# Attention with a gated MLP on one core: seventeen of 31 normalising products move from VectorE to GpSimd, and the planner's numbers are set anew

## The chip, the cores and the metric

The kernel runs on one core of one Trainium2 chip. The metric is device time in microseconds (us) of one execution, and lower is better. Several engines of the core work side by side, each through its own list of instructions in order: TensorE (PE) for matrix products, ScalarE (ACT) for activation functions, VectorE (DVE) and GpSimd (POOL) for elementwise work, SyncE (SP) for issuing DMAs. They meet only at semaphores.

## The reference

Attention with 32 heads of 20 columns over 2048 tokens, an MLP with the mish activation, and a gate per token that mixes the two:

```python
def _A_ref(x, wqkv, wo):
    B, S, D = x.shape                      # 1, 2048, 640
    H = 32; Dh = D // H
    qkv = ((x @ wqkv).reshape(B, S, 3, H, Dh)).transpose(2, 0, 3, 1, 4)
    q, k, v = qkv[0], qkv[1], qkv[2]
    p = softmax(einsum("bhqd,bhkd->bhqk", q, k) * Dh ** -0.5)
    o = einsum("bhqk,bhkd->bhqd", p, v)
    return o.transpose(0, 2, 1, 3).reshape(B, S, D) @ wo

def _B_ref(x, w1, b1, w2):                 # 640 -> 1536 -> 640
    h = x @ w1 + b1
    return (h * tanh(softplus(h))) @ w2

g = sigmoid((x * gate_w).sum(-1, keepdims=True))
out = g * _A_ref(x, wqkv, wo) + (1 - g) * _B_ref(x, w1, b1, w2)
```

All inputs are bf16.

## The kernel before

**Tiling.** The queries are cut into four blocks of 512 (`c`), the heads into eight groups of four (`g`), the keys into 16 tiles of 128. One unit is one head's score block: 128 keys by 512 queries, one matmul (L1204). There are 2048 units, and they go in slots of three, 683 slots in all. PE writes the three score blocks of a slot into one of two halves of six PSUM banks. ACT takes the exponential of all three in one instruction, 128 × 1536 (L1226), into one of six buffers `ETS`, and PE multiplies them by the values and sums them in the accumulator bank (L1463). The scores of slot s+2 need the half that slot s has left.

**Off-loaded units.** In about three slots of five, DVE takes the third unit: ACT's exp is then short, 128 × 1024, and DVE *evicts* the third block out of PSUM (`emit_x`, helper `dve_by`, L1271) as int16 numbers whose bits approximate an exponential. Up to four such units make a batch, and a batch needs three further DVE steps in SBUF (`close`): a bit operation on 2048 columns (`fraction`, L1335), a product (`times_y`, L1339, in one piece of 2048 or two of 1024) and a second bit operation (`power`, L1343). So each off-loaded unit shortens ACT's work and lengthens DVE's. Which slots have one is decided by `choose`, which weighs what DVE still owes (`late`, `urgent`, `other`) against limits such as `BEHIND` and `IDLE`, with a correction per eight slots from the table `NUDGE`.

**Normalising.** After the last key tile of a group (c, g), `group_done` (L1500) copies the accumulator to `OUNG` (L1552), which also holds the softmax sums. A DMA collects the sums in `RR`, DVE inverts them (`invert`, L1574), a DMA writes them to DRAM, and four DMAs spread them over the partitions in `BCT` (`spread`, L1581). Then one product, `OUNG` by `BCT`, 128 × 512 in fp32 to bf16, gives the normalised output in `OTN` or, for the later half of the queries, in `QT` (`times`, L1513). There are 31 of these products; the last two half groups take another way. The next group's copy to `OUNG` must wait for the product. The output projection (L1048) reads the products of all eight groups.

**The MLP.** Its tanh runs on ACT (L983, 24 pieces of 128 × 1024), the polynomial behind it on DVE in eight pieces (`mish`, L1005 and L1008).

**What sets the order.** A planner in Python writes all five instruction lists. It keeps a planned clock for each engine (`pl.now`), gives every instruction a planned cost (`WIDE` 0.60, `QUICK` 0.335, `EXP` 1.335, ...) and adds waits from the dependencies. Work of PE beside the scores (projections, MLP) stands in `tasks` with due slots; some are forced. DVE's work falls into two sorts: evictions out of PSUM, placed at once, and pieces in SBUF, kept in queues (`norm` for normalising, `soon` for batches, `blend` for the MLP, `bg`) from which `work` takes the next whenever the planned clock leaves room before the next eviction. GpSimd has only set-up work at the start and one addition at the end.

A second list of instructions for inputs that the approximation doesn't cover stands behind a flag and isn't run here.

## Time and profile before

| | us |
|---|---|
| median of three runs | 789.43 (788.85 to 789.61) |
| the profiled execution | 789.46 |
| its span, first to last instruction | 787.6 |
| mean granted TensorE clock | 0.998 of full speed |

The span is what the views below cut up; 1.9 us of the profiled execution lie outside of it. A view by groups gives for each group of instructions its line, engine, operation, tiles written and read with shapes, count, then busy time and the mean of one in ns, then the engine's idle time before them and who ended it. A timeline row is start, duration, engine, line, operation, tiles, count. L-numbers are lines of the kernel before. Consecutive instructions of ACT and of DVE overlap a little in the records, since each is recorded until its last result has been written.

DVE's 31 normalising products, and the POOL work that there is:

```profile
L1513 DVE TENSOR_TENSOR QT<-OUNG,BCT 128x512 bf16<-128x512 f32 x15 | 10.2, 681 | 0.0
L591 POOL MEMSET QT<- 128x2048 bf16 x7 | 12.3, 1808 | 0.0
L554 POOL MEMSET V_all<- 128x512 bf16 x1 | 2.4, 2361 | 0.0
BCT<-SUMS SPq DMA_DIRECT2D x124, 64.0 KB, 2.1
```

The last row is the spreading of the reciprocals: 124 DMAs, each landing 2.1 us after its issue in the median.

### The profile page before, as it was taken

What the parts mean: (1) busy time and instruction counts of PE and PEld (TensorE: products, weight loads), DVE (VectorE), ACT (ScalarE), POOL (GpSimd) and SP (SyncE); (2) the same over time, 40 slices, a digit from 0 to 9 for tenths busy, and PEclk for the clock granted to TensorE, in tenths of its full rate; (3) what the DMA queues carried; (4) which work ended last, traced back from release to release, by engine and by line L of the source; (5) the groups of instructions that cost most, each with busy time, mean ns of one, the idle gap of its engine ahead of it and who ended that gap; (6) DMA issues with size and microseconds to landing.
All of it is one profiled execution on the core that took longest, in us unless ns stands there. A gap on an engine that the chain in (4) does not pass through costs nothing.

```text
span 787.6 us, 16572 instructions
## 1 busy us (share of the span) xinstructions
PE 721.0 (92%) x6711; PEld 264.4 (34%) x6711; DVE 754.4 (96%) x1358; ACT 771.0 (98%) x715; POOL 20.3 (3%) x21
## 2 busy tenths in 40 slices
PE   8999999989899988999999999899989999989996
PEld 4333333233223333233333333333333333333332
DVE  4899999999999999999999999999999999999996
ACT  6999999999999999999999999999999999999995
POOL 8100000000000000000000000000000000000000
PEclk9999999999999999999999999999999999999999
DMA  8221310311233212402131201301121212101101
GB/s 188 75 60 53 100 54 15 94 59 53 66 104 84 65 51 73 129 15 52 52 80 51 69 22 51 85 16 45 47 85 50 82 44 56 32 23 28 25 20 39
DMA packets 77800, 47.13 MB, mean 60 GB/s; under 512 B 23916, under 2 KB 73700, under 8 KB 77668
## 3 DMA queue, kind: packets, MB, share of 16 engines
q1 hardware_dynamic: 77316, 45.80, 21.3%
q8 instruction: 56, 0.92, 0.5%
q14 instruction: 28, 0.23, 0.1%
q10 hardware_dynamic: 288, 0.16, 0.1%
q0 software_dynamic: 112, 0.01, 0.1%
HBM read 36.26 MB, written 7.52 MB: 56 GB/s over the span
## 4 chain that ended last, share of the span: by engine, by line
ACT 93%; PE 3%; DVE 3%; issue 0%; ACTq 0%
ACT ETS L1226 91%; ACT REG L983 2%; ACT W2R L983 1%; PE PS L1204 1%; PE PS L1463 1%; PE PS L562 0%; DVE HB L1054 0%; PE PS L1048 0%; PE PS L745 0%; PE PS L758 0%; PE PS L606 0%; DVE W2R L1054 0%; PE PS L950 0%; DVE QT L1271 0%; DVE QT L1513 0%
## 5 line engine op out<-in xcount | busy, mean ns | idle before, releaser
L1226 ACT ACTIVATE ETS<-PS 128x1024 bf16<-128x1024 f32 (+1 forms) x683 | 751.3, 1362 | 3.0 <-PE PS L1204 2.8
L1204 PE MATMUL PS<-QT,KT 32*128 32x512 bf16 (+1 forms) x2132 | 269.8, 378 | 53.0 <-ACT ETS L1226 42.7
L1463 PE MATMUL PS<-ETS,V_all 128*21 128x512 bf16 (+1 forms) x1690 | 166.5, 375 | 0.5 <-DVE OUNG L1552 0.5
L1204 PEld LDWEIGHTS PS<-QT,KT 32*128 32x128 bf16 x2132 | 67.5, 91 | 274.9 <-ACT ETS L1226 245.3
L1024 PE MATMUL PS<-W2R,HB 128*128 128x320 bf16 x384 | 69.0, 302 | 0.1
L1271 DVE TENSOR_SCALAR PADS<-PS 128x512 int16<-128x512 f32 x89 | 60.5, 683 | 6.8 <-PE PS L1204 6.5
L1271 DVE TENSOR_SCALAR QT<-PS 128x512 int16<-128x512 f32 x94 | 64.0, 683 | 2.2 <-PE PS L1204 1.6
L1271 DVE TENSOR_SCALAR OTN<-PS 128x512 int16<-128x512 f32 x89 | 60.4, 681 | 0.7 <-PE PS L1204 0.4
L950 PE MATMUL PS<-XB,REG 128*128 128x256 bf16 x360 | 55.1, 275 | 2.1 <-DVE XB L1031 0.9
L1463 PEld LDWEIGHTS PS<-ETS,V_all 128*21 128x21 bf16 x1690 | 42.5, 90 | 42.3 <-issue 26.3
L1008 DVE TENSOR_TENSOR U<-U 128x1024 f16<-128x1024 f16 x72 | 48.8, 677 | 0.1
L1024 PEld LDWEIGHTS PS<-W2R,HB 128*128 128x128 bf16 x384 | 30.9, 97 | 33.7 <-issue 19.7
L950 PEld LDWEIGHTS PS<-XB,REG 128*128 128x128 bf16 x360 | 29.0, 97 | 29.3 <-issue 27.0
L1271 DVE TENSOR_SCALAR REG<-PS 128x512 int16<-128x512 f32 x49 | 33.3, 683 | 0.7 <-PE PS L1204 0.5
L960 DVE TENSOR_TENSOR HB<-PS,B1T 128x512 bf16<-128x512 f32 x48 | 32.7, 682 | 0.8 <-PE PS L950 0.4
L1005 DVE TENSOR_SCALAR U<-U 128x1024 f16<-128x1024 f16 x72 | 30.0, 417 | 0.3
L1271 DVE TENSOR_SCALAR KT<-PS 128x512 int16<-128x512 f32 x40 | 27.3, 683 | 0.3
L1775 PE MATMUL PS<-KT 128*128 128x512 bf16 x88 | 25.1, 383 | 0.0
L1048 PE MATMUL PS<-WOQ,QT 128*128 128x320 bf16 x128 | 23.8, 302 | 0.8 <-DVE W2R L1054 0.3
L1048 PE MATMUL PS<-WOQ,OTN 128*128 128x320 bf16 x128 | 23.8, 302 | 0.2 <-issue 0.2
L667 PE MATMUL PS<-XB,REG 128*128 128x512 bf16 x80 | 23.2, 383 | 0.2 <-DVE WOQ L676 0.2
L1463 PE MATMUL PS<-QT,V_all 128*21 128x512 f16 x197 | 22.8, 384 | 0.4 <-DVE OUNG L1552 0.4
(188 smaller groups left out, 827.8 us busy)
## 6 DMA issues: line engine op xcount, KB each, us to landing
REG<-in_B_w_dram SPq DMA_DIRECT2D x36, 320.0 KB, 3.2
BCT<-SUMS SPq DMA_DIRECT2D x124, 64.0 KB, 2.1
W2R<-in_B_w_dram SPq DMA_DIRECT2D x12, 320.0 KB, 3.3
KT<-KS SPq DMA_DIRECT2D x28, 128.0 KB
QT<-QS SPq DMA_DIRECT2D x112, 20.0 KB
QS<-WOQ SPq DMA_DIRECT2D x16, 128.0 KB, 1.8
KS<-OTN SPq DMA_DIRECT2D x16, 128.0 KB, 1.7
W2R<-in_B_w_dram SPq DMA_DIRECT2D x1, 1920.0 KB, 8.3
```

Of the source, the lines that this page charges most:

```text
L950: return lambda e, bank: e.matmul(PS[:, bank, i * HW:(i + 1) * HW], w1b(n1)[:, f, i * P:(i + 1) * P], xt(c)[:, f, cols], start=(f == 0), s ...
L960: ev = dve(lambda e: e.tensor_tensor(hb, PS[:, bank, :].rearrange("p (i t) -> p i t", i=2), bias, ALU.add), [last, b_load, *guarded, *b_re ...
L983: ex = pl.add("act", lambda e: e.activation(U, h, AF.Tanh, scale=0.5, bias=-MISH_AT), [ev, u_free[0]], cost=0.95)
L1005: return lambda e: e.tensor_scalar(dst, src, *ops)
L1008: return lambda e: e.tensor_tensor(dst, one, two, ALU.mult)
L1024: return lambda e, bank: e.matmul(PS[:, bank, 0:HALF], HB[:, hc % 2, f, t * P:(t + 1) * P], W2[:, f, half * HALF:(half + 1) * HALF], start ...
L1048: return lambda e, bank: e.matmul(PS[:, bank, 0:HALF], otn(c, g, fast)[:, t * P:(t + 1) * P], WOG[:, g, half * HALF:(half + 1) * HALF], st ...
L1204: op = pl.add("pe", lambda e, i=i, g=real(g), tile=tile, j=j, cols=cols, c=c, of_q=of_q: e.matmul(scores(s)[:, i, cols], KT[32 * j:32 * j ...
L1226: e_op[s] = pl.add("act", lambda e: e.activation(ETS[:, s % NETS, 0:n, :], scores(s)[:, 0:n, :], AF.Exp, scale=SCALE, bias=LIFT if fast el ...
L1271: ev = dve_by(lambda e: e.tensor_scalar(block(batch["y"], n, I16), scores(s)[:, 2, :], SCALE * ULPS, BIAS, ALU.mult, ALU.add), [s_op[s], * ...
L1463: lasts[n] = pl.add("pe", lambda e, v=v, j=j, src=src[:, cols], of_q=of_q, count=count: e.matmul(PS[32 * j:32 * j + EW, ACC, of_q], v, src ...
L1775: pl.add("pe", lambda e: e.matmul(PS[:, bank, :], k[:, 0:P], k, start=True, stop=True), [free], cost=PASS, kind="S")
```

## The change

1. **A second home for a product.** `times` takes an engine. Each normalising product that waits in `norm` carries a second job for POOL, with a planned cost `ASIDE` of 1.3. After every DVE instruction that an eviction brings (in the helpers `dve` and `dve_by`), a new function `settle` looks back over DVE's planned line to the last SBUF piece (marked "L"). If the product, started behind that piece and behind its own inputs, ends by the planned end of the evictions that follow (less `APART`), it is put on POOL, with a wait for the last DVE instruction planned before its start.
2. **Patience.** While `patient` says so, DVE itself doesn't take a product until its planned clock is `AWAIT` = 3 past the product's input, except in the last 60 slots. The same mechanism is written for the short pieces of `mish`, but with `AWAIT_1` = 0 it is off there.
3. **A smaller debt.** Where the planner sums what DVE owes, a product that might go to POOL counts with 0.3 of its cost (`load`, `SHARE`).
4. **Numbers set anew.** `OLD`, `RISK` for POOL, `GIVE_BACK`, `SLOW_LOAD`, `SPARE`, `LEAD`, the planned cost of POOL's memsets, the planned landing time of the fetches of K and Q (`FETCH`), and 68 of the entries of `NUDGE`, which had 86 and has 87.

```diff
-OLD = 3
+OLD = 4
...
+ASIDE = 1.3
+ASIDE_1 = 1.2
+APART = 0.1
+AWAIT = 3
+SHARE = 0.3
+AWAIT_1 = 0
+CALM_END = 60
...
-RISK = {"pe": 0.1, "act": 0.3, "dve": 0.5, "pool": 1.2, "sp": 0.6}
+RISK = {"pe": 0.1, "act": 0.3, "dve": 0.5, "pool": 0.3, "sp": 0.6}
...
-GIVE_BACK = 40
+GIVE_BACK = 20
...
-SLOW_LOAD = 5.0
+SLOW_LOAD = 3.5
...
-SPARE = 7
+SPARE = 3.5
...
-LEAD = 5
+FETCH = (2.3, 3.0)
+LEAD = 10
-NUDGE = [0, 0, 0, 0, 0, 0, 0, 0, 0, 0, ...
+NUDGE = [0, -1.5, 0, 0.7, 0, 0.7, -3, 0.7, -1.5, 0, ...
...
-            return pl.add("dve", fn, deps, cost=cost, kind=kind)
+            op = pl.add("dve", fn, deps, cost=cost, kind=kind)
+            settle()
+            return op
+
+        def settle():
+
+            while fast:
+                for todo in (blend, norm):
+                    job = todo[0][5] if todo and len(todo[0]) > 5 else None
+                    ready = job and job[0]()
+                    if not ready:
+                        continue
+                    line = pl.line
+                    i = len(line)
+                    while i and not line[i - 1][2]:
+                        i -= 1
+                    begin = max(ready.t1 + HOP, pl.now["pool"], line[i - 1][0])
+                    while i < len(line) and line[i][0] <= begin:
+                        i += 1
+                    if begin + job[1] + APART <= pl.now["dve"]:
+                        todo.popleft()
+                        job[2](line[i - 1][1])
+                        break
+                else:
+                    return
+
+        def patient(op, wait):
+
+            return now["step"] < NSLOT - CALM_END and pl.now["dve"] < op.t1 + wait
+
+        def load(job):
+
+            return job[0] * (SHARE if len(job) > 5 else 1)
...
-            urgent, other = (sum(t[0] for todo in some for t in todo) for some in ((norm, *soon), (blend, bg)))
+            urgent, other = (sum(load(t) for todo in some for t in todo) for some in ((norm, *soon), (blend, bg)))
...
-            def times(src, deps):
-                oung_free[0] = bc_read[0] = otn_done[(c, g)] = pl.add("dve", lambda e: e.tensor_tensor(
-                    otn(c, g, fast), src, BC, ALU.mult), [*deps, *reads()], cost=WIDE)
+            def times(src, deps, eng="dve"):
+                oung_free[0] = bc_read[0] = otn_done[(c, g)] = pl.add(eng, lambda e: e.tensor_tensor(
+                    otn(c, g, fast), src, BC, ALU.mult), [*deps, *reads()], cost=WIDE if eng == "dve" else ASIDE, kind="L")
...
-                norm.append((WIDE, lambda: times(src, wide), lambda: wide[-1]))
+                norm.append((WIDE, lambda: times(src, wide), lambda: False if fast and patient(wide[-1], AWAIT) else wide[-1],
+                             0, None, (lambda: wide[-1], ASIDE, lambda dep: times(src, [*wide, dep], "pool"))))
```

What it does to the lists is read from the two programs. In the rows below the names are the tiles written and read, the numbers those of the first output; the lines of the changed kernel lie some 40 further on (L1271 becomes L1316, L1204 becomes L1249, L1513 becomes L1560, L606 becomes L649, L822 becomes L865, L1463 becomes L1510).

DVE at the product of the eleventh group, before:

```order
L1343 TENSOR_SCALAR PADS<-PADS 128x2048
L1271 TENSOR_SCALAR QT<-PS 128x512
L1335 TENSOR_SCALAR W2R<-QT 128x2048
L1271 TENSOR_SCALAR QT<-PS 128x512
L832 CAST V_all<-PS 128x3x8x20
L837 COPY OUTT<-PS 128x3
L1513 TENSOR_TENSOR OTN<-OUNG,BCT 128x512
L1271 TENSOR_SCALAR QT<-PS 128x512
L1339 TENSOR_TENSOR W2R<-W2R,QT 128x1024
```

DVE at the same product in the change:

```order
L1053 TENSOR_TENSOR U<-U 128x1024
L1050 TENSOR_SCALAR U<-U 128x1024
L1316 TENSOR_SCALAR PADS<-PS 128x512
L1316 TENSOR_SCALAR QT<-PS 128x512
L719 CAST WOQ<-PS 128x512
L1316 TENSOR_SCALAR PADS<-PS 128x512
L1053 TENSOR_TENSOR U<-U 128x1024
L1382 TENSOR_SCALAR W2R<-QT 128x2048
```

and POOL's list, with the semaphores that each waits for:

```order
L641 COPY REG<-OUTT 128x5 [waits f_gw]
L1560 TENSOR_TENSOR OTN<-OUNG,BCT 128x512 [waits f_dve,f_nr2] x4
L1739 TENSOR_LOAD FLAG
L1739 ISA x2
L1560 TENSOR_TENSOR OTN<-OUNG,BCT 128x512 [waits f_dve,f_nr2] x8
L1560 TENSOR_TENSOR QT<-OUNG,BCT 128x512 [waits f_dve,f_nr2] x5
L1952 TENSOR_TENSOR HB<-PADS,W2R 128x320 [waits f_act]
```

The product is gone from DVE's row; on POOL it waits for the L1050 piece above, and while it runs DVE has four reads of PSUM before its next SBUF piece. `f_dve` is DVE's count, `f_nr2` the landing of the spread reciprocals. Of the 31 products 17 stand on POOL, 14 on DVE.

PE around slots 99 to 104 (L1204 scores, L606 query projection, L822 V projection, L1463 value matmuls), before:

```order
L1204 MATMUL PS<-QT,KT 128x512 x3
L606 MATMUL PS<-XB,WOQ 128x512 x2
L1204 MATMUL PS<-QT,KT 128x512 x3
L1463 MATMUL PS<-W2R,V_all 21x512 x4
L1463 MATMUL PS<-ETS,V_all 21x512 x3
L1463 MATMUL PS<-KT,V_all 21x512 x4
L1463 MATMUL PS<-ETS,V_all 21x512 x4
L1204 MATMUL PS<-QT,KT 128x512 x3
L822 MATMUL PS<-REG,XB 128x160 x15
L1204 MATMUL PS<-QT,KT 128x512 x6
```

and in the change:

```order
L1249 MATMUL PS<-QT,KT 128x512 x3
L1510 MATMUL PS<-QT,V_all 21x512 x4
L1510 MATMUL PS<-ETS,V_all 21x512 x2
L1510 MATMUL PS<-KT,V_all 21x512 x4
L1249 MATMUL PS<-QT,KT 128x512 x3
L1510 MATMUL PS<-ETS,V_all 21x512 x7
L865 MATMUL PS<-REG,XB 128x160 x9
L1249 MATMUL PS<-QT,KT 128x512 x3
L865 MATMUL PS<-REG,XB 128x160 x6
L1249 MATMUL PS<-QT,KT 128x512 x6
```

The fifteen V matmuls stand as nine and six with a group of scores between.

PE near the start, slots 13 to 18, before:

```order
L1204 MATMUL PS<-QT,KT 128x512 x3
L1463 MATMUL PS<-ETS,V_all 21x512 x7
L795 MATMUL PS<-REG,XB 128x80 x20
L1204 MATMUL PS<-QT,KT 128x512 x3
L606 MATMUL PS<-XB,WOQ 128x512 x5
L1204 MATMUL PS<-QT,KT 128x512 x6
```

and, some slots earlier, in the change:

```order
L1510 MATMUL PS<-ETS,V_all 21x512 x7
L649 MATMUL PS<-XB,WOQ 128x512 x5
L1249 MATMUL PS<-QT,KT 128x512 x6
L649 MATMUL PS<-XB,REG 128x512 x5
L1249 MATMUL PS<-QT,KT 128x512 x3
```

The query projection (five matmuls from `WOQ`) stands ahead of a V piece and a K projection that it followed before. On ACT, 411 exps are short and 272 long (407 and 276 before), and three short ones follow each other 51 times instead of 30.

More of the change, by code (lines that the diff above doesn't have):

```diff
@@ L159, in __init__ @@
         self.passes = deque()
+        self.line = []
         self.queue = 0.0
@@ L590, in attention @@
             pad(1, 0)
-            q_blank = [pl.add("pool", lambda e, g=g: e.memset(QT[:, g, :], 0.0), cost=1.1) for g in range(1, NG)]
+            q_blank = [pl.add("pool", lambda e, g=g: e.memset(QT[:, g, :], 0.0), cost=1.8) for g in range(1, NG)]
             b_load = pl.add("pool", lambda e: e.dma_start(
@@ L1376, in tight @@
                 left = ends / TAKEN * EXP
-                before = sum(t[0] for t in blend if t[3] < pl.now["act"] + left)
+                before = sum(load(t) for t in blend if t[3] < pl.now["act"] + left)
                 return (late + urgent + before) * CROWD + need + MARGIN >= left
@@ L1754, in backlog @@
         def backlog():
-            return max(0.0, pl.now["dve"] - pl.now["act"]) + sum(t[0] for todo in (norm, *soon, blend, bg) for t in todo)
+            return max(0.0, pl.now["dve"] - pl.now["act"]) + sum(load(t) for todo in (norm, *soon, blend, bg) for t in todo)
         def pv_ready():
```

32 lines of the change are left out of this document (19 added, 13 removed).

## The prediction

> **What bounds the kernel now.** I read the page first: busy times, then the chain that ended last.
>
> ```profile
> span 787.6 us, 16572 instructions
> PE 721.0 (92%) x6711; PEld 264.4 (34%) x6711; DVE 754.4 (96%) x1358; ACT 771.0 (98%) x715; POOL 20.3 (3%) x21
> ACT 93%; PE 3%; DVE 3%; issue 0%; ACTq 0%
> ```
>
> ScalarE (ACT) is busy for 98% and makes 93% of the chain; VectorE (DVE) is close behind, GpSimd (POOL) is empty. The second view is busy time by stretch, to see whether one stage has slack (columns: stretch, its length, then busy time and count for PE, weight loads, DVE, ACT, POOL; clock, DMA).
>
> ```profile
> 40.00:120.00 80.00, 74.85 (x784) 28.23 (x782) 76.64 (x132) 79.55 (x76) 0.00 (x0) 1.00 0.22 64
> 120.00:240.00 120.00, 109.92 (x1012) 38.57 (x1002) 118.30 (x212) 119.65 (x112) 0.00 (x0) 1.00 0.24 69
> 600.00:720.00 120.00, 110.03 (x972) 41.25 (x972) 119.17 (x219) 120.00 (x110) 0.00 (x0) 1.00 0.17 46
> sum 769.00, PE 710.49 PEld 258.11 DVE 745.32 ACT 766.57 POOL 12.46; mean PE 88.81 PEld 32.26 DVE 93.16 ACT 95.82 POOL 1.56
> ```
>
> No stage is slack. ACT sets the end, with DVE 1 to 3 us behind it per 120 us, so the two questions are how much ACT work the change leaves and how much time ACT loses between its instructions. The groups of ACT by shape, and rows from the timeline that give the true pitch:
>
> ```profile
> L1226 ACT ACTIVATE ETS<-PS 128x1024 bf16<-128x1024 f32 x407 | 443.2, 1191 | 0.8 <-PE PS L1204 0.8
> L1226 ACT ACTIVATE ETS<-PS 128x1536 bf16<-128x1536 f32 x276 | 439.0, 1615 | 2.2 <-PE PS L1204 2.0
> 60.40 2.08 ACT L1226 ACTIVATE ETS<-PS 128x1024 bf16<-128x1024 f32 x2
> 61.30 1.18 ACT L1226 ACTIVATE ETS<-PS 128x1024 bf16<-128x1024 f32 x1
> 650.08 2.84 ACT L1226 ACTIVATE ETS<-PS 128x1536 bf16<-128x1536 f32 x2
> 651.41 1.51 ACT L1226 ACTIVATE ETS<-PS 128x1536 bf16<-128x1536 f32 x1
> ```
>
> One record overlaps the next by 0.28 us, so the means are not the pitch. Two undisturbed short exps take 2.08, one 1.18: pitch 0.90 (starts 60.40 and 61.30). Two long ones take 2.84, one 1.51: pitch 1.33. A slot in which DVE takes one of the three score blocks costs ACT 0.43 us less. The exps alone need 407 × 0.904 + 276 × 1.331 = 735.3 us (0.904 from the starts to three digits). What surrounds them:
>
> ```profile
> 9.39 16.09 ACT ETS L1226 x14
> 199.98 0.94 ACT W2R L983
> 769.63 8.88 ACT L1226 ACTIVATE ETS<-PS 128x1024 bf16<-128x1024 f32 x7
> ```
>
> The first exp starts at 9.39, the last ends at 769.63 + 8.88 = 778.51: 769.1 us. Less 735.3, less the 24 tanh pieces of the MLP at 0.94 (22.6) and the last record's overlap (0.3), ACT loses 10.9 us in all. That is the whole room for a better order; 9.4 us lie before and 9.1 after, outside of it. Only a part shows as idle:
>
> ```profile
> ACT ETS L1226 <- PE PS L1204: 2.8, 5, 1.0
> 28.89 1.45 ACT L1226 ACTIVATE ETS<-PS 128x1536 bf16<-128x1536 f32 x1 [0.25 <-PE PS L1204]
> 31.10 1.45 ACT L1226 ACTIVATE ETS<-PS 128x1536 bf16<-128x1536 f32 x1 [0.75 <-PE PS L1204]
> 118.70 3.28 ACT L1226 ACTIVATE ETS<-PS 128x1024 bf16<-128x1024 f32 x3 [0.45 <-PE PS L1204]
> 122.33 1.02 ACT L1226 ACTIVATE ETS<-PS 128x1024 bf16<-128x1024 f32 x1 [0.35 <-PE PS L1204]
> 29.48 0.39 PE L606 MATMUL PS<-XB,WOQ 128*128 128x512 bf16 x1 [0.63 <-DVE V_all L803]
> 120.75 1.21 PE L822 MATMUL PS<-REG,XB 128*128 128x160 bf16 x15
> ```
>
> ACT waits five times for scores, 2.8 us; four of these (1.8 us) lie at two places: a query projection that had to wait for a late V eviction (PE at 29.48), and fifteen V matmuls in one piece, 1.21 us against a short exp of 0.90 (PE at 120.75). The other 8 us are lateness below the 0.28 us overlap.
>
> **The change, part by part.** *Work taken from DVE.* Seventeen normalising products leave DVE. DVE's rows:
>
> ```profile
> 345.09 1.28 DVE L1271 TENSOR_SCALAR QT<-PS 128x512 int16<-128x512 f32 x2
> L1513 DVE TENSOR_TENSOR OTN<-OUNG,BCT 128x512 bf16<-128x512 f32 x16 | 10.9, 680 | 0.0
> L1339 DVE TENSOR_TENSOR OTN<-OTN 128x2048 f16<-128x2048 f16 x8 | 9.7, 1216 | 0.0
> L1339 DVE TENSOR_TENSOR QT<-QT 128x1024 f16<-128x1024 f16 x13 | 8.8, 680 | 0.1
> L1343 DVE TENSOR_SCALAR QT<-QT 128x2048 int16<-128x2048 int16 x18 | 12.2, 680 | 0.0
> L1343 DVE TENSOR_SCALAR QT<-QT 128x1024 int16<-128x1024 int16 x7 | 2.9, 419 | 0.0
> L1339 DVE TENSOR_TENSOR QT<-QT 128x512 f16<-128x512 f16 x3 | 1.3, 420 | 0.0
> L1343 DVE TENSOR_SCALAR QT<-QT 128x512 int16<-128x512 int16 x8 | 2.3, 286 | 0.0
> ```
>
> Two evictions in a row take 1.28 us and one 0.68, so the pitch is the record less 0.08. Removed: 17 × 0.60 = 10.2 us. By the two programs' instruction counts, evictions for off-loaded score blocks rise by 4 (4 × 0.60 = +2.4), and their batches are cut otherwise: products of 2048 +11 (+12.5), of 1024 −18 (−10.8), of 512 other than the moved ones −4 (−1.4); bit operations of 2048 +8 (+4.8), of 1024 −8 (−2.7), of 512 −8 (−1.6), together +0.8. Net DVE: −10.2 + 2.4 + 0.8 = −7.0 us.
>
> *Work taken from ACT.* 411 short exps and 272 long ones instead of 407 and 276: 4 × 0.427 = −1.7 us, directly on the path. This is the surest term.
>
> *Work given to POOL.* No row shows this product on POOL. The nearest are:
>
> ```profile
> L1904 POOL TENSOR_TENSOR HB<-PADS,W2R 128x320 bf16<-128x320 f32 x1 | 0.9, 862 | 755.8 <-ACT PADS L1902 755.8
> L598 POOL COPY REG<-OUTT 128x5 bf16<-128x5 bf16 x1 | 0.2, 206 | 3.5 <-DMA OUTT<-in_gate_w_dram 3.5
> 781.12 0.53 ACT L1902 ACTIVATE PADS<-PS,GATE 128x320 f32<-128x320 f32 x1 [2.61 <-PE PS L1048]
> 781.74 0.86 POOL L1904 TENSOR_TENSOR HB<-PADS,W2R 128x320 bf16<-128x320 f32 x1 [755.79 <-ACT PADS L1902]
> 780.64 2.37 DVE L1054 SCALAR_TENSOR_TENSOR HB<-PS,GATE,W2R 128x320 bf16<-128x320 f32 x5
> ```
>
> 320 columns take 0.86 us. All of it by size gives 0.86 × 512/320 = 1.38 us; with 0.21 fixed (the copy of 5 columns) it is 0.21 + 0.66 × 1.6 = 1.26. I take 1.3, plus 0.09 from release to start (781.65 to 781.74). POOL is idle, so the time itself is hidden; its cover is the row of PSUM reads that DVE makes meanwhile: 1.6 to 2.4 us in fourteen of the seventeen places (three or four reads at 0.60, or two and one of 320 to 480 columns), 1.17 and 1.20 in the sixth and eighth, and the last stands among the small transposes at the end. If the cover were gone the loss would be DVE's, not ACT's, as long as DVE has room.
>
> *The added waits.* On POOL each product waits for one DVE instruction and for the broadcast of the reciprocals; behind it stand only the next product, the flag's load and the tail's add. On DVE the next group's copy out of PSUM (L1599) waits for the product; at least seven DVE instructions stand between, about 4 us against 1.4, so I cost it at 0. Were it late, the accumulator bank would be freed late and PE's value matmuls would queue. The fourteen products left on DVE are now held back by a planned 3 us; nobody waits for them that soon, since the projection that reads them needs all eight groups of its block of queries. 0.
>
> The Trainium skill, page "SBUF — State Buffer", section "Who interferes with whom", speaks against the change: "A DVE instruction with two SBUF inputs contends with a GpSimd instruction that reads SBUF", and the later of the two stands still. No run here shows it, since the only such row above ran beside DVE instructions with one SBUF input. By that rule the two short rows cost DVE 2 × 0.25 us, and the sum below would be unchanged, since DVE has 7 us more to spare.
>
> *The order set anew.* The two places of the 1.8 us are both rewritten: the fifteen V matmuls now stand as nine and six around a group of scores, and the query projection is moved ahead of the V piece. Score groups that follow each other with nothing between, the mark of a PE that comes late, fall from 51 to 43 up to slot 670 in the program's order, but rise from three to four in slots 11 to 29, beside the first place. Bounds: −1.8 to 0; I take −1.4. Runs of three short exps rise from 30 to 51. PE works 721.0/683 = 1.06 us per slot on average, a short exp lasts 0.90, so a run of three lets PE fall 0.46 behind. If all of the hidden 8 us sat in the 30 old runs, each would cost 0.27, the 21 new ones 5.7; if none, 0. The 8 us spread evenly are 0.012 per slot, which is nearer to none, for most runs of the old order pass unharmed: I take +0.4. The tail loses one DVE product of 0.60 after the last eviction, but its final transpose follows ACT's last exp (778.51) and that exp's value matmuls anyway, by 0.6 us:
>
> ```profile
> 779.11 0.44 DVE L1536 STREAM_TRANSPOSE U<-PS 128x256 f32<-128x256 f32 x1
> ```
>
> So 0 there.
>
> *Sum*, on the profiled execution (787.6 span, 1.9 outside, 789.46; the runs' median is 789.43): −1.7 − 1.4 + 0.4 = −2.7, so 786.7.
>
> **The rivals.**
> *Count alone (12%).* The new order loses as much between exps as the old: 789.4 − 1.7 = 787.7. For it: 8 of the 10.9 us sit in no place that can be named.
> *PE lags in the longer runs (14%), slower.* One mechanism: a third short exp in a row finds its scores not ready. It decides once a new run costs more than 0.15 us (21 × 0.15 = 3.1, the two gains). At 0.27 it is 789.4 − 1.7 + 5.7 = 793.4, less the 1.4 if that holds: 792 to 793.4. Against it: four of ACT's five visible waits lie at the two named places, which leaves one for all 30 old runs together.
> *DVE and POOL in each other's way (10%), slower.* If the chip drifts from the plan, the product meets DVE's SBUF pieces instead of PSUM reads and one stands still for the other. Worst 17 × 1.3 = 22 us; half of it, 11, is 4 more than the 7 spared, in stages where DVE has 1 to 3 us per 120: 789.4 − 1.7 + 4 = 791.7. It decides from 0.4 us per product. Against it: the product is released by the DVE instruction that opens the row, so it starts in step with DVE even when the clock of the plan is off; only a late broadcast would break that. The sentence quoted from the Trainium skill speaks for this rival.
> *More slack recovered (8%).* DVE's 7 us also shorten the hidden lateness by a quarter: 786.7 − 2 = 784.7 or less.
> *The products stay on DVE:* no, the new program has them on POOL.
>
> **How the numbers follow.** Forecast 56%, its own range 785 to 788.2. Below 0.2% (1.6 us, about what a measurement of this kernel can tell from no change) counts as the same: 787.9 to 791.0. The forecast lies faster with 48 of its 56, count alone with 7 of 12, more slack with 8: 63%. Same: 8 + 5 and 3 from the mild ends of the slow cases: 16%. Slower: 21%. For 8 in 10 I cut the lowest tail and part of the slow cases: 783.6 to 791.2.
>
> **What would show it.** Right: 411 short exps; seventeen POOL rows of 1.3 us; L1599 with no wait on POOL; DVE near 747 us busy; no ACT waits near 120 us; ACT's list of waits at most 2 us. Wrong: DVE products of 2048 or 1024 over their 1.22 and 0.68 (ports); POOL rows over 1.6; ACT waits for scores after three short exps; a broadcast landing after the DVE instruction that should release the product.

## The result, and the profile after

| | before | changed |
|---|---|---|
| median, us (range) | 789.61 (788.85 to 789.78) | 786.44 (785.99 to 786.54) |
| executions | 5 | 5 |
| span of the profiled execution, us | 787.6 | 784.2 |
| short / long exps | 407 / 276 | 411 / 272 |
| first exp start to last exp end, us | 769.12 | 766.15 |

The ratio is 0.9961, 95% interval 0.995 to 0.9972. The forecast was 786.7, in a range of 783.6 to 791.2.

The page's span and busy lines of the changed kernel, to be held against those of before:

```profile
span 784.2 us, 16559 instructions
PE 718.3 (92%) x6701; PEld 262.2 (33%) x6701; DVE 748.8 (95%) x1326; ACT 769.1 (98%) x715; POOL 41.8 (5%) x38
ACT 93%; DVE 3%; PE 3%; issue 0%
```

The chain is unchanged: ACT sets the end. DVE's busy time fell by 5.6 us (754.4 to 748.8), ACT's by 1.9, while the span fell by 3.4. The groups by shape of ACT and POOL, and ACT's list of waits:

```profile
L1271 ACT ACTIVATE ETS<-PS 128x1024 bf16<-128x1024 f32 x411 | 445.1, 1213 | 0.5 <-PE PS L1249 0.5
L1271 ACT ACTIVATE ETS<-PS 128x1536 bf16<-128x1536 f32 x272 | 430.7, 1631 | 1.3 <-PE PS L1249 1.3
L1560 POOL TENSOR_TENSOR OTN<-OUNG,BCT 128x512 bf16<-128x512 f32 x12 | 15.2, 1268 | 364.5 <-DVE PADS L1386 113.0 <-DVE QT L1390 45.8 <-DVE KT L1382 44.5
L1560 POOL TENSOR_TENSOR QT<-OUNG,BCT 128x512 bf16<-128x512 f32 x5 | 6.3, 1268 | 357.5 <-DVE OTN L1382 154.1 <-DVE QT L1390 94.9 <-DVE U L1583 62.1
ACT ETS L1271 <- PE PS L1249: 1.9, 3, 1.0
```

The seventeen products are there and take 1.268 us each on POOL in the mean. What POOL waited for last, by these rows, is DVE's pieces in SBUF (L1382, L1386, L1390), as the plan wanted, not the broadcast of the reciprocals. The means of the exps (1213 and 1631 ns) are longer than before (1191 and 1615), but the pitch is not: the starts of two undisturbed short exps still lie 0.904 apart, and the last exp's own record grew by 0.06 with the others. A record's mean thus moves with no change of what it costs. ACT's visible waits for scores are three instead of five.

The long sum is therefore made from starts. For each exp, its start after the first exp, less the pitches of everything ACT did before it (0.904, 1.3305, 0.94 for a tanh piece), is the time lost so far. Cut at the 30th, 90th and 110th of the 683 exps (about 43, 107 and 129 us), the increments are, in us:

| time ACT loses | exps 1–30 | 31–90 | 91–110 | 111–683 | sum |
|---|---|---|---|---|---|
| before | 1.62 | 0.79 | 1.28 | 7.30 | 10.99 |
| changed | 1.43 | 0.59 | 0.60 | 7.04 | 9.66 |
| difference | −0.19 | −0.20 | −0.68 | −0.26 | −1.33 |

With four exps shorter (−1.71) this gives −3.04; the longer last record (+0.06) and rounding bring it to the −2.97 of the first table. The span fell by 0.5 more: 0.6 behind the last exp (9.13 to 8.54), less 0.1 ahead of the first. Four runs below with a stretch of 766.15 or nearly so had 8.5 to 9.2 behind it, so that half microsecond belongs to the execution.

### The profile page after: what moved, and what is told of

Read it like the earlier page. It is cut to its first block, busy times and chain, and to the rows that moved or that the text cites. A ratio compares the mean times of both kernels' runs of the same rounds, so it can differ in the third digit from the quotient of the medians.

```text
span 784.2 us, 16559 instructions
## 1 busy us (share of the span) xinstructions
PE 718.3 (92%) x6701; PEld 262.2 (33%) x6701; DVE 748.8 (95%) x1326; ACT 769.1 (98%) x715; POOL 41.8 (5%) x38
## 4 chain that ended last, share of the span: by engine, by line
ACT 93%; DVE 3%; PE 3%; issue 0%
ACT ETS L1271 90%; ACT REG L1026 2%; ACT W2R L1026 1%; PE PS L1249 1%; PE PS L1510 0%; PE PS L605 0%; PE PS L649 0%; DVE HB L1099 0%; DVE REG L1316 0%; DVE W2R L1099 0%; DVE OTN L1386 0%; PE PS L801 0%; PE PS L788 0%; DVE QT L1589 0%; PE PS L993 0%
## 5 line engine op out<-in xcount | busy, mean ns | idle before, releaser
L1271 ACT ACTIVATE ETS<-PS 128x1024 bf16<-128x1024 f32 (+1 forms) x683 | 749.9, 1379 | 1.9 <-PE PS L1249 1.9
L1249 PE MATMUL PS<-QT,KT 32*128 32x512 bf16 (+1 forms) x2125 | 269.1, 378 | 51.6 <-ACT ETS L1271 41.1
L1510 PE MATMUL PS<-ETS,V_all 128*21 128x512 bf16 (+1 forms) x1687 | 164.2, 375 | 0.0
L1249 PEld LDWEIGHTS PS<-QT,KT 32*128 32x128 bf16 x2125 | 67.2, 91 | 275.4 <-ACT ETS L1271 248.4
L1316 DVE TENSOR_SCALAR OTN<-PS 128x512 int16<-128x512 f32 x105 | 70.9, 681 | 1.7 <-PE PS L1249 1.4
L1316 DVE TENSOR_SCALAR PADS<-PS 128x512 int16<-128x512 f32 x88 | 59.9, 682 | 3.9 <-PE PS L1249 3.4
L1316 DVE TENSOR_SCALAR QT<-PS 128x512 int16<-128x512 f32 x91 | 62.0, 682 | 1.7 <-PE PS L1249 1.2
L1510 PEld LDWEIGHTS PS<-ETS,V_all 128*21 128x21 bf16 x1687 | 41.6, 90 | 40.4 <-issue 26.6
L993 PEld LDWEIGHTS PS<-XB,REG 128*128 128x128 bf16 x360 | 29.2, 97 | 27.3 <-issue 24.9
L1316 DVE TENSOR_SCALAR KT<-PS 128x512 int16<-128x512 f32 x51 | 34.7, 683 | 2.4 <-PE PS L1249 2.1
L1560 POOL TENSOR_TENSOR OTN<-OUNG,BCT 128x512 bf16<-128x512 f32 x12 | 15.2, 1268 | 364.5 <-DVE PADS L1386 113.0
L1050 DVE TENSOR_SCALAR U<-U 128x1024 f16<-128x1024 f16 x72 | 29.9, 415 | 0.3
L1560 POOL TENSOR_TENSOR QT<-OUNG,BCT 128x512 bf16<-128x512 f32 x5 | 6.3, 1268 | 357.5 <-DVE OTN L1382 154.1
```

The source lines that it names most:

```text
L993: return lambda e, bank: e.matmul(PS[:, bank, i * HW:(i + 1) * HW], w1b(n1)[:, f, i * P:(i + 1) * P], xt(c)[:, f, cols], start=(f == 0), s ...
L1050: return lambda e: e.tensor_scalar(dst, src, *ops)
L1249: op = pl.add("pe", lambda e, i=i, g=real(g), tile=tile, j=j, cols=cols, c=c, of_q=of_q: e.matmul(scores(s)[:, i, cols], KT[32 * j:32 * j ...
L1271: e_op[s] = pl.add("act", lambda e: e.activation(ETS[:, s % NETS, 0:n, :], scores(s)[:, 0:n, :], AF.Exp, scale=SCALE, bias=LIFT if fast el ...
L1316: ev = dve_by(lambda e: e.tensor_scalar(block(batch["y"], n, I16), scores(s)[:, 2, :], SCALE * ULPS, BIAS, ALU.mult, ALU.add), [s_op[s], * ...
L1510: lasts[n] = pl.add("pe", lambda e, v=v, j=j, src=src[:, cols], of_q=of_q, count=count: e.matmul(PS[32 * j:32 * j + EW, ACC, of_q], v, src ...
```

## The experiments

In all runs the kernel before was measured beside, at 789.31 to 789.37 in the median. Diffs are against the changed kernel unless another is named. "Stretch" is first exp start to last exp end of the profiled execution.

### The offload by itself: three runs

**e1: the changed order, the seventeen products back on DVE, in place.**

```diff
-                oung_free[0] = bc_read[0] = otn_done[(c, g)] = pl.add(eng, lambda e: e.tensor_tensor(
+                op = pl.add(eng, lambda e: e.tensor_tensor(
...
+                if eng == "pool":
+                    op.eng = op.key = "dve"
+                oung_free[0] = bc_read[0] = otn_done[(c, g)] = op
```

> The changed kernel's lists with one edit: the seventeen products run on VectorE again, each at the end of the row of evictions in which GpSimd had it; nothing else moves. 411 short exps as in the change, so the count theory alone (ACT's work sets the end, DVE has room) says 786.4, no difference from the change. If DVE's room was what the change bought, DVE carries 17 x 0.60 = 10.2 us more in a schedule that has 1 to 4 us of idle per 120 us: part of it comes out as later evictions, later scores and longer gaps between exps. Expected 789 to 794, 791 the likeliest; ACT's loss between exps up by 3 to 7 us.

788.01 us, ratio 0.9983 (0.9974 to 0.9992), stretch 767.71. The page's busy line and ACT's waits:

```profile
PE 717.2 (91%) x6701; PEld 262.3 (33%) x6701; DVE 755.6 (96%) x1343; ACT 770.3 (98%) x715; POOL 20.6 (3%) x21
ACT ETS L1271 <- PE PS L1249: 2.0, 4, 1.0
```

The stretch is 1.56 longer than with the offload, 0.09 per product. That is about half of the least that was expected (3 to 7 us). By the loss table (1.42, 1.06, 0.53, 8.22) it is spread over the second and the last column. Nothing of it shows in the list of waits, which has 2.0 us against 1.9. The rest of the gain (789.4 to 788.0) stays without any offload.

**e9: the kernel before, fourteen of its products moved to GpSimd in place.** Its lists are kept; each moved product waits for the DVE instruction ahead of a row of PSUM reads near its old place. Diff against the kernel before, in which `wides` collects the products:

```diff
+        def aside(op, row):
+            line = [o for o in pl.ops if o.eng == "dve"]
+            before = line[line.index(op) + (row - 1 if row > 1 else -1)]
...
+            op.eng = op.key = "pool"
+            op.deps.append(before)
+
+        if fast:
+            for n, row in ((1, 7), (4, 8), (5, 3), (6, 3), (7, 1), (13, 4), (14, 1), (15, 2), (16, 2), (17, 7),
+                           (20, 3), (23, 1), (27, 4), (28, 1)):
+                aside(wides[n], row)
```

> The kernel before with its five lists as they are, except that fourteen of its 31 normalising products go to GpSimd, each to start with the DVE instruction that opens a row of PSUM reads near the product's old place. No score block changes sides: 407 short exps. Theory (an in-place offload relieves lateness on DVE's path, about 0.09 us of ACT's time per product, as the run with the products back on DVE showed): ACT's stretch from first exp start to last exp end falls from 769.1 by 14 x 0.09 = 1.3 to about 767.8, the time from 789.4 to 788.1; the list of ACT's waits for scores is unchanged near 28 and 120 us. Rival (the 1.6 us of that run came from the changed order, which is tight for DVE, and the order before has no use for the freed time): 769.1 and 789.4 within 0.4, with DVE about 8 us less busy. Second rival (collisions with DVE's SBUF pieces): over 790.

789.74 us beside 789.35 before, ratio 1.0002 (0.9993 to 1.0011), stretch 768.56. Busy line and POOL's groups:

```profile
PE 720.4 (91%) x6711; PEld 263.5 (33%) x6711; DVE 747.7 (95%) x1344; ACT 771.0 (98%) x715; POOL 37.9 (5%) x35
L1514 POOL TENSOR_TENSOR OTN<-OUNG,BCT 128x512 bf16<-128x512 f32 x8 | 10.1, 1268 | 371.9 <-DVE REG L1336 140.5 <-DVE HB L960 69.5 <-DVE KT L1340 58.0
L1514 POOL TENSOR_TENSOR QT<-OUNG,BCT 128x512 bf16<-128x512 f32 x6 | 7.6, 1266 | 315.0 <-DVE OTN L1344 106.1 <-DVE OTN L1336 71.1 <-DVE OTN L1272 67.7
```

DVE is 6.7 us less busy, and no product is held up (1268 and 1266 ns). Two DVE pieces in SBUF are, by little: a bit operation at 173.39 takes 0.86 instead of 0.68, a product of 2048 columns 1.33 instead of 1.22. The time is the same: the interval reaches from 0.6 us faster to 0.9 slower, and the 1.3 us of the theory lie outside. The stretch did fall by 0.56, more than the 0.4 that the rival allowed, but in two jumps: 0.41 at one wait for a DMA (told below) and 0.15 near 443 us, which is also gone in e11, where no product is moved. The theory of 0.09 us per product, wherever it is moved, falls.

**e10: four more products of the changed kernel to GpSimd, 21 in all,** by the same function:

```diff
+            for n, row in ((5, 1), (8, 2), (9, 8), (10, 2)):
+                aside(wides[n], row)
```

> The changed kernel with its lists as they are, except that four more of the fourteen products that were left on DVE go to GpSimd (21 in all), each released by the DVE instruction before a row of PSUM reads. Theory (about 0.09 us of ACT's time per product): ACT's stretch falls from 766.15 by 4 x 0.09 = 0.4 to about 765.8, the time to 786.1. Rival (DVE's lateness is used up where it cost something): 766.15 within 0.1 and 786.4. Second rival (collisions): DVE's SBUF pieces over their usual duration and the stretch over 766.3.

786.18 us, ratio 0.9957 (0.9944 to 0.9971), stretch 766.14. DVE's busy time fell to 747.4, and every column of the loss table reads as in the changed kernel within 0.01. The interval overlaps that of the change.

The three together: in these runs DVE's time was worth something only to the order that was planned with it. The changed order counts on the seventeen products being gone and loses 1.6 us when they return (e1); the old order has no use for the relief (e9), and the new none for more of it (e10).

### What GpSimd's reads cost DVE: three runs

**e2: the release taken away.** Each product starts as soon as the reciprocals' broadcast is there, in a row of PSUM reads or not.

```diff
+                if eng == "pool":
+                    op.deps.remove(deps[-1])
```

> The changed kernel's lists, but each GpSimd product no longer waits for the VectorE instruction that opens the row of evictions: it starts when the spread reciprocals have landed, wherever DVE then is. Theory that GpSimd and DVE stand in each other's way for SBUF: products meet DVE pieces with two SBUF inputs or on 1024 and 2048 columns of 16 bits, and one of the two stands still; in the change one such meeting is on record (L1589 took 944 ns instead of 420). Some 12 of 17 collide at 0.3 to 1.2 us each, 4 to 12 us more DVE time: 788 to 793, 790 the likeliest, with DVE records of these lines over 1.2 us or POOL records over 1.6. Rival, that the place does not matter: 786.4 and all POOL records at 1.27.

791.39 us, ratio 1.0026 (1.0017 to 1.0035), 5.0 more than the change. (The profiled execution, 794.28, is the longest of eleven; the lowest is 789.73.) POOL's groups, three collisions out of the timeline, and ACT's waits:

```profile
L1560 POOL TENSOR_TENSOR OTN<-OUNG,BCT 128x512 bf16<-128x512 f32 x12 | 17.0, 1420 | 359.9 <-DMA BCT<-SUMS 359.9
L1560 POOL TENSOR_TENSOR QT<-OUNG,BCT 128x512 bf16<-128x512 f32 x5 | 8.1, 1622 | 360.6 <-DMA BCT<-SUMS 360.6
...
97.89 1.26 POOL L1560 TENSOR_TENSOR OTN<-OUNG,BCT 128x512 bf16<-128x512 f32 x1 [23.61 <-DMA BCT<-SUMS]
98.23 1.48 DVE L1382 TENSOR_SCALAR KT<-HB 128x2048 int16<-128x2048 int16 x1
...
216.37 1.27 POOL L1560 TENSOR_TENSOR OTN<-OUNG,BCT 128x512 bf16<-128x512 f32 x1 [24.06 <-DMA BCT<-SUMS]
216.46 2.25 DVE L1386 TENSOR_TENSOR W2R<-W2R,PADS 128x2048 f16<-128x2048 f16 x1
...
263.94 0.42 DVE L1386 TENSOR_TENSOR PADS<-PADS,QT 128x512 f16<-128x512 f16 x1
263.98 2.04 POOL L1560 TENSOR_TENSOR OTN<-OUNG,BCT 128x512 bf16<-128x512 f32 x1 [22.84 <-DMA BCT<-SUMS]
...
ACT ETS L1271 <- PE PS L1249: 5.8, 14, 1.0
```

At 216.46 a product of 2048 columns takes 2.25 us where it usually takes 1.21, and ends 1.07 behind the end of POOL's instruction (217.64): nearly all of it was done after that. At 98.23 the bit operation, with one SBUF input, takes 1.48 instead of 0.68. At 263.94 DVE was first, and POOL's instruction, which also stood through the two short SBUF pieces that followed (to 264.90), took 2.04 instead of 1.27. Sixteen of the seventeen products meet a DVE piece in this way, and DVE is busy for 759.3 us instead of 748.8. Aligned, all seventeen pass in 1.26 to 1.28. DVE's lateness comes through as waits of ACT: 5.8 us in 14 instead of 1.9 in three, and the loss table's last column goes from 7.04 to 13.27.

**e5: nothing read on GpSimd.** Each of the seventeen products is replaced by a write of zeros of the same size, so the kernel leaves out the normalising of seventeen of the 31 groups.

```diff
-                oung_free[0] = bc_read[0] = otn_done[(c, g)] = pl.add(eng, lambda e: e.tensor_tensor(
+                oung_free[0] = bc_read[0] = otn_done[(c, g)] = pl.add(eng, lambda e: e.memset(
+                    otn(c, g, fast), 0.0) if eng == "pool" else e.tensor_tensor(
```

> The changed kernel's lists and waits, but each of GpSimd's seventeen products is replaced by a write of zeros to the same tile (the normalised output of these groups is left out of the result): GpSimd reads nothing and is busy for about 0.5 instead of 1.27 us. It is the ceiling of what the offload could give at this order. Theory that the aligned products cost DVE nothing, but for the one meeting at the end (L1589, 944 instead of 420 ns): the same as the change within its noise, 785.9 to 786.6, with L1589 back at 420 ns. Rival, that the products still cost DVE time that the records do not show (delayed starts): 1 us or more below the change, 785.4 or less.

786.10 us, ratio 0.9958 (0.9944 to 0.9972), stretch 766.15, as in the change. One collision is left in the changed kernel, at the end; its rows, and behind the dots those of the same place here:

```profile
768.34 1.27 POOL L1560 TENSOR_TENSOR QT<-OUNG,BCT 128x512 bf16<-128x512 f32 x1 [62.09 <-DVE U L1583]
768.94 0.94 DVE L1589 TENSOR_TENSOR QT<-U 128x256 bf16<-128x256 f32 x1
```

```profile
768.19 0.53 POOL L1560 MEMSET QT<- 128x512 bf16 x1 [62.82 <-DVE U L1584]
768.82 0.42 DVE L1590 TENSOR_TENSOR QT<-U 128x256 bf16<-128x256 f32 x1
```

In the first fence (changed) DVE's small product takes 0.94; in the second (e5) it starts behind the zeros, which are written by 768.72, and takes 0.42. The 0.52 cost ACT nothing: the stretch is the same.

**e6: that last product released after the small one.**

```diff
+                if eng == "pool" and end_done:
+                    op.deps.append(end_done[-1])
```

> The changed kernel with one wait altered: the last GpSimd product starts behind the half group's own product (L1589) instead of beside it. L1589 falls from 944 to about 420 ns. If that meeting sets the end, the tail and the time fall by 0.5 us: 785.9. If ACT's last exp and its value matmuls set the end, as the two finishing within 0.6 us of each other suggests, 0 to 0.2 us: 786.3. I expect the latter.

786.57 us, ratio 0.9964 (0.995 to 0.9977), stretch 766.15. The small product is at 0.43; the bit operation behind it now takes 1.58 instead of 0.68, and the time doesn't move. The collision was passed on here, not removed; in e5 it was removed, and the stretch is 766.15 in both and in the change. So interference between POOL and DVE costs the changed kernel nothing that these runs can see.

The Trainium skill, page "SBUF — State Buffer", section "Who interferes with whom", has it that a DVE instruction with two SBUF inputs contends with a GpSimd instruction that reads SBUF but not with one that only writes, and that a one-input operation in a two-port mode contends as well. The runs agree on the readers: 2.25 against 1.21 and 0.94 against 0.42 for DVE's products, 1.48 against 0.68 for the one-input operation on 16-bit numbers. On the writers they are silent, since in none of them does a DVE instruction with two SBUF inputs run beside GpSimd's zeros.

### Code without numbers, numbers without code: three runs

**e3: the new code with the old numbers and the old table.**

```diff
-LEAD = 10
+LEAD = 5
...
-NUDGE = [0, -1.5, 0, 0.7, 0, 0.7, -3, 0.7, -1.5, 0, ...
+NUDGE = [0, 0, 0, 0, 0, 0, 0, 0, 0, 0, ...
```

> The new code with the old numbers (reserves, thresholds, planned costs, table): eleven products on GpSimd, 402 short exps, five fewer than before the change. If the offload is what gains, the time falls below before by DVE's 11 x 0.60 us worth of room: 787 or less. If the count of short exps decides, 5 x 0.43 = 2.1 us more: 791.5. I expect 791, between 789.5 and 793.

**e4: the new numbers and the new table without the code.**

```diff
...
-            op = pl.add("dve", fn, deps, cost=cost, kind=kind)
-            settle()
-            return op
...
+            return pl.add("dve", fn, deps, cost=cost, kind=kind)
...
```

> The kernel before with the new numbers and no offload: 397 short exps, ten fewer than before. By the count 10 x 0.43 = 4.3 us more, 793.7. If the new numbers mend the order by themselves (fetch times, the place of the query projection, the V matmuls in two pieces), 1 to 2 us less than that. I expect 793, between 791 and 795.

**e7: the changed kernel with all 87 corrections at zero.**

```diff
-NUDGE = [0, -1.5, 0, 0.7, 0, 0.7, -3, 0.7, -1.5, 0, ...
+NUDGE = [0] * 87
```

> The changed kernel with all entries of the table NUDGE at zero, everything else new: 400 short exps, eight products on GpSimd. By the count 11 x 0.43 = 4.7 us over the change, 791.1; with the loss between exps at 12 to 14 us, as in the two runs with numbers not matched to their order, 793 to 795. I expect 793. That the offload alone makes the kernel faster than before would be 788 or less.

| | us | ratio (interval) | products on POOL | short exps | loss in the four columns |
|---|---|---|---|---|---|
| e3, code alone | 792.35 | 1.0037 (1.0023 to 1.0051) | 11 | 402 | 1.62, 0.80, 1.70, 7.71 |
| e4, numbers alone | 796.16 | 1.008 (1.0067 to 1.0094) | 0 | 397 | 1.43, 1.35, 0.59, 10.74 |
| e7, table at zero | 798.21 | 1.0112 (1.0097 to 1.0128) | 8 | 400 | 1.48, 1.27, 2.52, 8.08 |

The short exps by shape, of e3, e4 and e7:

```profile
L1271 ACT ACTIVATE ETS<-PS 128x1024 bf16<-128x1024 f32 x402 | 435.4, 1186 | 0.4 <-PE PS L1249 0.4
```

```profile
L1227 ACT ACTIVATE ETS<-PS 128x1024 bf16<-128x1024 f32 x397 | 427.2, 1175 | 2.5 <-PE PS L1464 1.4 <-PE PS L1205 1.1
```

```profile
L1271 ACT ACTIVATE ETS<-PS 128x1024 bf16<-128x1024 f32 x400 | 433.7, 1178 | 1.6 <-PE PS L1249 0.8 <-PE PS L1510 0.5
```

Each half makes the kernel slower than before, and so does the whole without its table. The planner puts fewer blocks on DVE (5, 10 and 7 fewer than before), and the order loses more as well. Two of the three came out slower than expected: e4 (791 to 795) loses 14.1 us between the exps; e7 (793 to 795) loses 13.4, as expected, but 11.8 us lie behind its last exp instead of 8.5, since PE waits there for DVE's last batch (2.24 us at 785.98). A table of corrections fits one set of numbers and one code. Whether the old code would gain as well from a table fitted anew to it wasn't tried. The third column is low in e4 (0.59) and e1 (0.53), which have the new numbers and table and no product on POOL, and high in e3 (1.70), which has neither numbers nor table, and e7 (2.52), which lacks the table. The gain near 120 us thus doesn't need the offload; it goes with the numbers and the table together.

### The two places of visible waits: three runs

**e8: at the first place (28 to 31 us) of the changed kernel, two score groups moved ahead of the work that held them up.**

```diff
+        if fast:
+            ahead(13, 3)
+            ahead(17, 14)
```

> The changed kernel with two groups of scores put ahead on PE at the two places where ACT still waits visibly: the group of slot 13 goes between the second and the third of five query projection matmuls, that of slot 17 behind the sixth of twenty V matmuls. If ACT sets the end and nothing else moves, ACT's waits of 0.29 and 0.55 us there go, and the time falls by 0.6 to 0.9 us: 785.7. If the gain is given back later (the delayed V and query evictions make DVE late), 786.4.

786.45 us, ratio 0.996 (0.9946 to 0.9973), stretch 766.17. ACT's rows there, in the changed kernel and then in e8:

```profile
24.94 4.63 ACT L1271 ACTIVATE ETS<-PS 128x1536 bf16<-128x1536 f32 x4 [0.29 <-PE PS L1249]
30.11 10.55 ACT L1271 ACTIVATE ETS<-PS 128x1024 bf16<-128x1024 f32 x10 [0.55 <-PE PS L1249]
```

```profile
29.82 3.30 ACT L1272 ACTIVATE ETS<-PS 128x1024 bf16<-128x1024 f32 x3 [0.15 <-PE PS L1250]
33.39 7.38 ACT L1272 ACTIVATE ETS<-PS 128x1024 bf16<-128x1024 f32 x7 [0.27 <-PE PS L1250]
```

The waits are smaller and the loss is the same: after the 20th exp 0.33 was saved (1.10 against 1.43), after the 40th nothing (1.55 against 1.52). The change had done likewise: before, 0.25 and 0.75 at 28.9 and 31.1, and now 0.29 and 0.55 at 24.9 and 30.1. By these rows PE has more work than fits there, and moving it moves the wait.

**e11: the kernel before with its fifteen V matmuls as nine and six.** **e12: the changed kernel with them in one piece again.** The diffs, against before and against the changed kernel:

```diff
+        if fast:
+            ahead(102, 6)
...
+        if fast:
+            behind(101, 6)
```

> The kernel before with one place of its order of PE's list altered: the fifteen V matmuls that stand in one piece (at 120.75 us) become nine and six around a group of three score matmuls, as in the changed kernel. Nothing else moves; 407 short exps. Theory (a wait that is removed here is kept, since ACT sets the end): the 0.35 us wait of ACT at 122.33, which loses 0.48, is gone, ACT's stretch from first exp start to last exp end falls from 769.12 to about 768.65, the time by 0.5 to 788.9. The wait at 118.70 (0.45, 0.63 lost) stays. Rival (given back, as at the first place in the run with the scores ahead): other waits near 123 to 130 us take its place and the stretch stays at 769.1 within 0.1.

> The changed kernel with one place of its order of PE's list altered: the nine and six V matmuls at 118.4 us stand as fifteen in one piece again, ahead of the score group that stood between them. Nothing else moves; 411 short exps, seventeen products on GpSimd. Theory (a V piece longer than a short exp makes ACT wait and the loss is kept): a wait of ACT for scores of 0.2 to 0.45 near 120 us, the stretch rises from 766.15 to 766.5 to 766.65, the time to 786.9. Rival (the changed kernel is far enough ahead there that the piece is absorbed, or the loss is made good later): no such wait or 766.15 within 0.1.

e11: 789.64 us, ratio 1.0004 (0.9995 to 1.0013), stretch 768.88. The third column reads 1.24 instead of 1.28. The wait at 122.33 is gone, with 0.42 gained, and between 124 and 126.2 us, where waits of 0.11 and 0.02 now stand, 0.47 is lost again: the rival. The 0.24 by which the stretch is shorter lie elsewhere, 0.10 at the wait of 118.70 and 0.15 near 443 us. e12: 786.45 us, ratio 0.9961 (0.9947 to 0.9975), stretch 766.95. The third column reads 1.02 instead of 0.60: the piece does cost 0.42, and it is kept to the end of that execution. ACT's row and PE's, of e12:

```profile
118.95 1.21 PE L865 MATMUL PS<-REG,XB 128*128 128x160 bf16 x15
120.54 11.89 ACT L1272 ACTIVATE ETS<-PS 128x1024 bf16<-128x1024 f32 x11 [0.41 <-PE PS L1250]
```

The five times of e12 run from 785.89 to 787.25 (the profiled one is the longest, and also lost 0.38 more in the first column), so the median doesn't confirm the 0.42. The same piece thus costs 0.42 in one order and nothing in the other. A likely reason is what surrounds it. The time from 40 to 120 us by engines, of the changed kernel, against the first row of that view in the prediction:

```profile
40.00:120.00 80.00, 76.77 (x801) 29.61 (x798) 76.33 (x137) 80.00 (x76) 3.80 (x3) 1.00 0.23 68
```

PE does 76.77 us of work there, where before it did 74.85. If PE is behind at that point in the kernel before, cutting the piece only passes the lateness on; this is argued from the two rows, not tried.

What the larger of the two old waits was is told by e11, whose lists are those of before up to that place. SP's row that fetches the queries and PE's row of the late scores, before; SP's row of the changed kernel; PE's rows of e11 and of e9, which has the old order too:

```profile
112.42 3.15 SPq L658 DMA_DIRECT2D QT<-QS  x8
...
118.27 0.39 PE L1204 MATMUL PS<-QT,KT 32*128 32x512 bf16 x3 [0.65 <-ACT ETS L1226]
```

```profile
108.91 3.33 SPq L701 DMA_DIRECT2D QT<-QS  x8
```

```profile
118.00 0.39 PE L1205 MATMUL PS<-QT,KT 32*128 32x512 bf16 x3 [0.55 <-DMA QT<-QS]
...
118.18 0.39 PE L1205 MATMUL PS<-QT,KT 32*128 32x512 bf16 x3 [0.24 <-DMA QT<-QS]
```

The scores waited until the fetch of the next queries had landed: eight transfers, the first issued at 112.42. In the trace of before the same idle time of PE stands under ACT's name, but the semaphore events in it tell the two apart. The last landing that these scores wait for came at 118.13, and PE started 0.14 later; in e11 it came at 117.86 and in e9 at 118.05, and PE started 0.14 and 0.13 later. Counted from the first exp, the landing was 0.10 sooner in e11 and 0.40 sooner in e9 than before, and ACT's next exp came 0.10 and 0.41 sooner. That is why ACT waited 0.04 in e9 instead of 0.45; why the fetch took less time in that execution (5.3 us from the first issue instead of 5.7) is left open. The change issues the fetch 3.5 us earlier, it has landed by 113.14, and the wait isn't there; which of the change's numbers does that wasn't tried.

## Why the prediction was right, and where its steps were off

**The fewer long exps** (−1.7) are as forecast: 411 and 272, and the pitch unchanged. This is more than half of the gain, and of the sets tried only code, numbers and table together get it: neither half does (e3, e4).

**The two places** (−1.4 forecast) brought −0.19 and −0.68, −0.87 in all: a term that was sized too large, with one of its two causes wrong. At the first place the wait wasn't removed but moved (0.29 and 0.55 instead of 0.25 and 0.75), as the warning about three to four groups in a row had it. At the second I put both waits down to the fifteen V matmuls. Only the smaller, 0.35, belongs to them; the larger, 0.45, was a fetch of queries that landed late, and in the change this fetch lands 5 us earlier. The new numbers for the fetches stood in the change, and I had given them no term.

**The longer runs of three short exps** (+0.4 forecast) cost 0.66. Outside the two places, the third exp of such a run and the exp behind it lose 2.19 us in 46 runs, where before they lost 1.53 in 25. The +0.4 was a choice between 0 and 5.7, 0.02 per new run, and the 0.012 per slot beside it doesn't give it (three slots in each of 21 runs would be 0.76). The runs show 0.03 per new run; the rival of a lagging PE needed 0.15.

**DVE's relief** has no term in the sum, and this is the step that failed. All the other exps outside the two places lose 1.1 us less together (5.45 instead of 6.56), and nothing in the forecast stands for that. In e1, the same order without the relief, they lose 6.60 again, and the runs of three 2.68 instead of 2.19. The relief is thus worth 1.56 us to the changed order, and nothing that shows to an order that doesn't count on it (e9) or has had enough of it (e10). The rival "more slack recovered" (784.7) had the mechanism, with 2 us for it. "Count alone" at 787.7 is what the changed order gives without the offload, 788.0 in e1.

The four terms are −1.7, −0.9, +0.7 and −1.1, which give the −3.0 of the stretch. That the forecast sum of −2.7 stands so close is in part luck: the places were 0.5 too hopeful, the runs 0.3 too cheap, and a gain of 1.1 was left out.

**DVE's net work** was forecast as −7.0 and measured −5.6. The pieces are as counted, but DVE now pauses 173 times instead of 153, and the last record before a pause shows its 0.08 of overlap: 20 × 0.08 = 1.6. With it the forecast is 749.0, measured 748.8. (A pause is counted where a DVE instruction starts behind the end of the one before.) In e9 it accounts for 1.1 of the 1.7 by which 14 × 0.60 = 8.4 misses the 6.7: there are 167 pauses. The two pieces held up there are 0.3 more.

**POOL's product** took 1.26 to 1.28 us in every aligned place, within the 1.26 to 1.38 of the prediction. The two short rows of 1.17 and 1.20 us, for which the rule quoted in the prediction gave 0.25 us each, showed no collision. The first of them, in the timeline:

```profile
194.40 1.27 POOL L1560 TENSOR_TENSOR OTN<-OUNG,BCT 128x512 bf16<-128x512 f32 x1 [23.87 <-DVE HB L1382]
194.44 0.66 DVE L875 CAST V_all<-PS 128x480 bf16<-128x480 f32 x1 [0.18 <-PE PS L865]
195.02 0.68 DVE L1316 TENSOR_SCALAR KT<-PS 128x512 int16<-128x512 f32 x1
195.62 1.21 DVE L1386 TENSOR_TENSOR HB<-HB,W2R 128x2048 f16<-128x2048 f16 x1
```

The row of reads is 1.18 us from start to start, the product 1.27, and the SBUF product behind it still takes its 1.21: an overlap of 0.05 us costs nothing that shows here.

**The added waits** cost nothing: L1599, the copy that waits for POOL's product, has no idle time put down to POOL. **The tail** cost nothing, though its one collision took 0.52 us of DVE.

**The rival of DVE and POOL in each other's way** (791.7) is what the kernel becomes without the release: 791.39 in e2. DVE's 10.5 us more in the profiled execution are close to the 11 that the rival took. The reason given against it, that the product starts with DVE and not by the clock, is the one that decided.

## What to carry to other kernels

Work that was moved off an engine that isn't the bound gained nothing here by itself (e9); it gained where the order was planned again and used the freed time for the engine that sets the end (e1 against the change). What an engine's relief is worth can then be tried directly: put the work back and leave the order alone. A table that was fitted to an order belongs to that order: judge a rule and its table together, and compare a new rule only with a table fitted to it. A wait at one place is worth its length only if the engine behind it has room afterwards; sum the lateness from starts past the place before counting a gain.

## What the runs showed of the hardware

- A GpSimd product and two kinds of DVE instruction hold each other up, in both directions and for nearly the whole of the other's time: DVE's products with both inputs in SBUF (2.25 us instead of 1.21 for 2048 columns), and its one-input operations on 16-bit numbers in SBUF (1.48 instead of 0.68), which were new to the prediction. GpSimd's own product took 2.04 instead of 1.27 where DVE came first. DVE's reads of PSUM ran on at 0.60 from start to start beside the aligned products (195.02 to 195.62), also where their second input was in SBUF (the product from `PS` and `B1T` at 550.00: 0.60), and so did its transpose of fp32 numbers in SBUF (0.45 at 768.46).
- GpSimd's product costs 2.11 ns per column and 0.19 us besides, from 0.862 us for 320 columns (the sum at the end of the kernel before) and 1.268 for 512; my bounds of 1.26 and 1.38 had guessed 0.21 and 0 for the fixed part. The Trainium skill, page "GPSIMD Engine Reference", section "Elementwise — side-by-side cycle accounting", has about 2.6 cycles per element for two inputs, at 1.2 GHz an estimate of 2.17 ns, and the trace agrees within 3%.
- Profiled executions of kernels with the same lists of PE and ACT repeat to 0.01 us of lateness over long stretches: changed, e5, e6 and e10 read 1.43 to 1.44, 0.59, 0.60 and 7.04 to 7.05 in the loss table. Where they part (0.38 in e12's first column, far ahead of its edit), it is in jumps at single waits.
